# An S4 layer with a gated feed-forward on one core: the same 2006 tasks in another order

## The chip, the core and the metric

The kernel runs on one core of a Trainium2 chip. The metric is the device time of one execution in microseconds. It is read beside a profile of one further execution, which gives what each engine did: TensorE (PE, matrix products), VectorE (DVE), ScalarE (ACT), GpSimd (POOL) and SyncE (SP), which here does nothing but issue DMA transfers.

## The reference, cut to what matters

```python
x = A_u                                            # 2048 tokens x 448 channels
sa, ca, ga, sb, cb, gb = (silu(c) @ w_mod) in six parts
h = layernorm(x) * (1 + ca) + sa
# S4 convolution of h, channel by channel
dt = exp(log_dt)
K = real(einsum("dn,dnl,dn->dl", C, exp(dt * A * l), dt * B))   # 256 states, 2048 taps
y = irfft(rfft(pad(h)) * rfft(pad(K)))[:2048] + h * Dskip
x = x + ga * y
h = layernorm(x) * (1 + cb) + sb
# GeGLU: 448 -> 1792 -> 448
x = x + gb * ((gelu(h @ w_gate) * (h @ w_up)) @ w_down)
```

## The kernel before, in words

**Stages.** The kernel has four parts that overlap in time.

1. *Normalisation and transform of the input.* The input is normalised (tasks `bn`, `norm`), and its Fourier transform over the 2048 taps is made in two matrix stages (`ua`, `ub`) with evictions from PSUM (`ua.ev`, `ub.ev`) and a trip through DRAM between them.
2. *Generation of the convolution kernel.* The 448 channels are cut into 56 pieces of 8, each with 256 states. A piece needs two exponential factors (PE tasks `x.mm` L638 and `y.mm` L657 with ACT exponentials L644 and L662), angles (`ang`, `anc`, PE L675), their magnitude (`mag`: ACT L680 or DVE L683), sine and cosine on ACT (L688, L692, L699), two products on DVE (`tx` L721, 1.22 us; `tyc` L725, 2.29 us) and then the generation matmuls on PE (`kgen`, L748). Two pieces make one tile that is evicted (`kev`, ACT or DVE), corrected with the skip term (`kd`, L766), transformed by PE (`ka`, L771) and evicted again (`kout`, ACT or DVE). The coefficients that this needs come from a chain of small DVE and ACT operations on `in_abc` (tasks `p.*`), turned through DRAM.
3. *The convolution.* For two of three channel groups PE transforms the kernel (`f.fwd`, L1094), DVE multiplies with the input's transform (`f.pr`, L1098), PE transforms back (`f.inv`, L1105), and the result goes to DRAM. The third group is done at the end by other shapes (`t.fwd` L1189, DVE combinations `t.p0`, `t.p1` at L1197 and L1200, `t.inv` L1207, `t.i0` L1216, stores L1224 and turned reads `yi.l0`, `yi.l1` at L1297). The last inverse stage, token block by token block, is `co.mm*` (PE, L1404 and L1409) with the residual and second normalisation behind it.
4. *The feed-forward*, for four blocks of 512 tokens and 14 tiles of 128 hidden channels. A task `gu` (PE L1530, with a 64-row part at L1524) makes gate and up of one tile; ACT applies the GELU (L1537), DVE multiplies (L1544), and the hidden values are split in a high and a low half (L1556, L1559). The down products (`dn`, PE L1599 and L1630) follow after each block. The gate/up weights are split once (`w.hi`, `w.lo`), kept in DRAM as `w_d`, and for blocks 1 to 3 read back by `wr.ld` (L1367, 896 KB each, on SP) into a ring of three slots; one load serves two `gu` tasks. The down weights arrive by `d.ld` and `e.ld` (L1737) and share a ring of two buffers (`fq`) with the products of gate and up.

**What sets the order.** Every piece of work is a task. A task is added with a name, the engines that can do it, a function that issues its instructions, and the tasks it depends on. A table `PLACE` gives each task a rank, one number for the whole kernel; where a task can run on several engines a letter behind the rank picks one (a ACT, d DVE, p POOL, s SP). `Plan.order` (with an assertion that every task stands behind those it depends on) sorts by rank, and `Plan.run` lets the tasks issue their instructions in that order:

```python
    def order(self):
        out = sorted(self.tasks, key=lambda t: t.at)
```

Each engine takes its instructions strictly in the order in which they were issued to it. So the rank sets, at the same time, the order on every engine, which buffer of a ring a task gets, and in which order transfers enter SP's queue. The ranks are no times: an engine waits in front of a task until its inputs and its buffer are there, and everything behind it on that engine waits too. Instructions of PE come in several tile shapes (rows by columns of the array that a matmul uses): 64x128 for `x.mm`, `y.mm` and `ang`, 128x32 for `kgen`, 128x64 for `ka` and `co.mm*`, 128x128 for the transforms and most of `gu`.

Of the kernel before, what the change touches and what calls it, by code (L numbers as in the profile page):

```python
# [40 lines left out]
    "anc": "120 138 145 163 157 200 209 244 266 311 327 339 347 355 438 456 470 487 499 524",  # L41
    "ang": "108 112 126 149 151 169 204 212 241 298 319 324 341 350 421 443 454 476 496 506 511 591 602 610 654 670 690 698 "
        "741 761 764 775 792 795 805 885 894 905 908 927 932 950 1007 1018 1021 1034 1039 1051 1115 1124 1135 1151 1157 1169 "
        "1187 1197",
    "as": "67d 80a 99d 109d 114d 128d 156a 185a 250d 258d 265a 289d 309d 333d 334d 365d",
    "bn": "48 49 60 58 41 50 51 53 227 243 235 239 187 224 197 210",
    "c.ai": "1257",
    "c.ak": "5",
    "c.au": "4",
    "c.c": "2",  # L50
    "c.ea": "20",
    "c.ih": "1283",
    "c.ld": "7",
    "c.rd": "22",
    "c.t1": "219",
    "co.adde": "1329 1347 1366 1355",
    "co.addl": "1384 1387 1421 1410",
    "co.addx": "1495 1510 1499 1522 1676 1716 1739 1688 1799 1811 1817 1809",
    "co.ca": "1404a 1408a 1456a 1441a",
    "co.cb": "1415d 1416a 1459a 1448a",  # L60
    "co.h0": "1398a 1403a 1447d 1430a",
    "co.h2": "1534a 1579a 1571a 1561a 1752a 1748d 1759a 1765d 1856d 1889a 1841a 1873a",
    "co.l0": "1402 1405 1449 1434",
    "co.l2": "1541 1584 1573 1576 1753 1754 1763 1766 1857 1893 1851 1884",
    "co.mme": "1321 1341 1336 1346",
    "co.mml": "1381 1382 1409 1407",
    "co.mmx": "1492 1506 1494 1509 1640 1703 1735 1649 1792 1805 1812 1796",
    "co.n": "1392 1399 1438 1425",
    "co.nx": "1527 1574 1548 1532 1749 1746 1751 1764 1829 1875 1837 1870",
    "co.rc": "1390 1397 1431 1423",  # L70
    "co.rcx": "1525 1743 1828",
    "co.rt": "1388 1393 1424 1418",
    "co.rtx": "1524 1741 1818",
    "co.xt": "1541 1584 1573 1576 1753 1754 1763 1766 1857 1893 1857 1884",
    "co.ta": "1401 1406 1453 1436",
    "co.tb": "1411 1413 1454 1439",
    "cos": "523 609 623 635 689 694 715 708 760 774 794 791 804 819 817 893 906 912 930 946 949 963 1016 1028 1040 1050 1057 "
        "1066 1129 1134 1155 1175 1180 1196 1207 1220",
    "cos2": "124 146 147 167 165 207 213 254 273 321 332 342 349 359 445 462 485 492 502 531",
    "d.hi": "1566 1547 1583 1496 1533 1600 1504",  # L80
    "d.ld": "1555 1538 1569 1484 1516 1585 1491",
    "d.lo": "1567 1552 1587 1501 1535 1602 1514",
    "d0": "13",
    "dn": "1603 1605 1607 1613",
    "dn.k0": "1742 1891 1994",
    "dn.k2": "1755 1896 2000",
    "dn.k3": "1757 1899 2002",
    "dn.r": "1606 1608 1614 1634",
    "dn.r1": "1745 1963 2008",
    "dn.r4": "1768 1903 2004",  # L90
    "dn.r5": "1770 1909 2010",
    "dn.r6": "1778 1908",
    "dn.rh": "2005 2012 2016",
    "dn.s0": "2015",
    "dn.s1": "2017",
    "dn.st": "1657 1658 1620 1639 1747 1780 1775 1779 2007 1952 1950 1948 2014 2006 2013",
    "dn0": "1726 1737 1880 1885 1986 1992",
    "dn1": "1738 1887 1993",
    "dn2": "1767 1902 2003",
    "dn3": "1772 1905",  # L100
    "dn3h": "2009 2011",
    "dn4": "1750 1897 1999",
    "dn5": "1744 1894 1998",
    "dn6": "1761 1898 2001",
    "dsk": "178",
    "dt": "26",
    "e.f": "1666 1718 1704 1615 1650 1628 1685",
    "e.hi": "1668 1720 1708 1617 1653 1631 1689",
    "e.ld": "1656 1705 1696 1610 1638 1619 1675",
    "e.lo": "1671 1723 1710 1618 1655 1636 1691",  # L110
    "ev.end": "1253",
    "ev.fp": "707",
    "ev.geg": "1445",
    "ev.pq": "1328",
    "ev.ps": "1437",
    "ev.ub": "389",
    "ev.w0": "1339",
    "f.fc": "714 716 754 773 801 823 851 880 895 917 942 1015 1030 1052 1071 1094 1114 1137 1158 1189",
    "f.fwd": "738 753 783 806 832 855 879 902 924 947 969 998 1014 1036 1055 1077 1098 1120 1141 1162 1209 1216",
    "f.inv": "750 768 796 815 847 865 889 911 936 960 983 1010 1026 1046 1067 1089 1108 1130 1154 1176 1226 1232",  # L120
    "f.pr": "743 759 790 812 839 859 884 907 931 953 975 1002 1020 1041 1060 1083 1101 1125 1149 1167 1212 1225",
    "f.st": "763 782 809 830 897 878 904 929 977 1000 1009 1023 1042 1079 1090 1106 1131 1148 1168 1193 1243 1240",
    "f.ut": "710 721 755 776 803 826 854 870 901 918 944 966 988 1017 1032 1054 1073 1097 1123 1138 1160 1182",
    "f.z": "758a 778d 802a 829a 868a 871d 896d 926a 952d 979a 1005d 1019a 1038d 1061a 1085a 1102a 1128d 1143a 1163a 1188a "
        "1235a 1239a",
    "gs": "70 110",
    "gu": "1480 1497 1511 1519 1528 1539 1549 1560 1570 1578 1596 1616 1622 1632 1644 1651 1660 1669 1678 1686 1694 1706 "
        "1712 1721 1777 1781 1784 1798 1800 1808 1816 1822 1830 1838 1843 1852 1859 1869 1907 1910 1913 1919 1924 1931 1935 "
        "1941 1945 1958 1964 1970 1974 1981",
    "gu.g": "1429 1450 1458 1465 1468 1471 1474 1481 1502 1508 1521 1529 1540 1550 1562 1572 1581 1595 1604 1623 1633 1641 "  # L130
        "1654 1661 1670 1679 1687 1695 1709 1713 1722 1727 1782 1785 1793 1801 1806 1813 1824 1831 1839 1844 1853 1860 1874 "
        "1878 1911 1914 1920 1925 1932 1936 1942 1946 1959 1965 1972 1975 1982 1987",
    "gu.h0": "1475 1485 1515 1536 1557 1580 1599",
    "gu.ha": "1626 1647 1663 1682 1698 1717 1730 1787 1804 1819 1835 1849 1864 1882 1917 1933 1943 1953 1967 1977 1989",
    "gu.hs": "1629 1646 1667 1690 1701 1732 1734 1794 1820 1826 1846 1862 1871 1888 1923 1930 1955 1957 1983 1979 1996",
    "gu.l0": "1478 1488 1517 1544 1558 1582 1601",
    "gu.la": "1635 1648 1672 1684 1700 1725 1733 1789 1825 1834 1855 1854 1866 1883 1918 1939 1956 1961 1968 1984 1990",
    "gu.ls": "1630 1652 1673 1693 1702 1740 1736 1797 1821 1840 1850 1865 1872 1890 1929 1940 1971 1960 1995 1980 1997",
    "gu.m": "1432 1452 1460 1466 1469 1472 1476 1483 1505 1513 1526 1531 1545 1554 1564 1575 1591 1597 1609 1625 1637 1643 "
        "1659 1662 1674 1681 1692 1697 1711 1715 1724 1729 1783 1786 1795 1803 1807 1815 1827 1833 1842 1847 1858 1863 1876 "  # L140
        "1881 1912 1916 1921 1927 1934 1938 1944 1949 1962 1966 1973 1976 1985 1988",
    "gu.s": "1627 1645 1664 1683 1699 1719 1731 1788 1810 1823 1836 1848 1867 1886 1922 1928 1951 1954 1969 1978 1991",
    "gu2": "1420 1427 1442 1457 1464 1467 1470 1473",
    "ka": "216 272 306 363 374 409 465 519 570 606 711 719 745 800 836 887 920 954 957 989 1063 1070 1127 1174 1190 1224 "
        "1245 1250",
    "kd": "205 249 304 352 371 403 459 515 559 582 675 697 742 789 820 883 913 939 951 984 1047 1068 1119 1172 1185 1211 "
        "1241 1248",
    "kev": "191d 238d 285d 351d 368d 401d 431d 497a 551d 579d 661a 680d 737d 786a 816a 856a 890d 922a 948d 980d 1045d 1065a "
        "1104d 1146a 1183d 1198a 1219a 1246a",
    "kgen": "142 175 189 223 257 280 294 322 329 357 387 396 418 424 480 491 513 546 534 574 620 641 659 673 724 731 757 779 "  # L150
        "788 810 828 841 857 874 898 916 933 941 965 974 1003 1029 1043 1059 1081 1100 1117 1139 1145 1164 1181 1195 1204 "
        "1213 1238 1242",
    "kout": "247a 288a 318a 377d 448a 414a 505a 530a 583d 634d 720d 733d 771a 811a 843a 892d 928a 962a 992a 993d 1076a 1110d "
        "1142a 1177a 1200a 1228a 1251d 1252a",
    "lt0": "55 136 317 358 568 766 860 955",
    "lt1": "87 173 335 393 696 833 971 995",
    "m.cp": "532d 589a 818d",
    "m.cp0": "40d",
    "m.ev": "63 68 47 545 598 838",
    "m.ld": "6 19 12 423 539 727",  # L160
    "m.mm": "45 57",
    "m.mq": "527 581 772",
# [1671 lines left out]
```

## Time and profile before

| what | value |
|---|---|
| median of 3 runs | 787.75 us (787.74 to 788.98) |
| profiled execution, its own time | 787.92 us |
| span of the profiled execution | 786.1 us |
| mean granted TensorE clock | 0.991 |
| busy: PE, DVE, ACT | 728.7, 591.4, 460.1 us |
| moved by DMA | 139.88 MB |

How to read it: the span is the time from the first to the last recorded instruction. Busy time is what an engine spent on instructions; its share of the span is an average over stages with different limits, so the prediction reads it by stretches of 40 us. The chain of waits starts at the last instruction and goes back at each step to what released it. The ends of matmuls are modelled, and instructions in a row overlap in the list by 0.07 to 0.16 us, so that sums of durations come out a little above the time they take.

### The profile page before, as it was taken

How to read it: one execution, taken by the hardware profiler on the slowest of the kernel's cores; microseconds unless marked ns; L12 is line 12 of the kernel's file. 1: busy time of each engine (PE TensorE's matmuls, PEld its weight loads, DVE VectorE, ACT ScalarE, POOL GpSimd, SP SyncE). 2: the span in 40 equal slices, each digit the busy share in tenths (PEclk: the TensorE clock that was granted, in tenths of full speed). 3: DMA queues.
4: the chain of work that ended last, by engine and by line, in shares of the span. 5: the costliest groups of instructions: out<-in, count | busy, mean ns of one | idle time of the engine just before them, and what ended most of it. 6: DMA issues, size and time to landing. Idle time of an engine off the chain costs nothing.

```text
span 786.1 us, 19037 instructions
## 1 busy us (share of the span) xinstructions
PE 728.7 (93%) x8166; PEld 445.2 (57%) x8166; DVE 591.4 (75%) x891; ACT 460.1 (59%) x613; POOL 9.0 (1%) x24
## 2 busy tenths in 40 slices
PE   1876889998899999989999999999999999999998
PEld 0333454543667767778784445444595446944478
DVE  4889999999999999988768851469773587134743
ACT  5699999899999999961554730233421244012320
POOL 0000000000000000000300000000000000000000
PEclk9899999999999999999999999999999999999999
DMA  9555558997887767999797884345437324012201
GB/s 265 157 156 145 155 140 249 277 277 227 240 259 216 224 190 216 285 300 251 192 312 221 274 219 146 129 134 186 161 67 213 104 94 134 14 48 94 82 2 60
DMA packets 103791, 139.88 MB, mean 178 GB/s; under 512 B 34388, under 2 KB 85268, under 8 KB 103706
## 3 DMA queue, kind: packets, MB, share of 16 engines
q1 hardware_dynamic: 97828, 130.47, 56.7%
q10 hardware_dynamic: 5318, 7.22, 2.9%
q8 instruction: 64, 1.05, 0.5%
q0 software_dynamic: 560, 0.98, 0.4%
q14 instruction: 21, 0.17, 0.1%
HBM read 100.39 MB, written 36.01 MB: 174 GB/s over the span
## 4 chain that ended last, share of the span: by engine, by line
PE 67%; ACT 13%; DVE 9%; DMA 7%; issue 3%; SPq 1%; ACTq 0%; DVEq 0%
PE pq L1530 29%; PE pq L1630 9%; PE pd L1599 4%; PE kg L748 3%; PE pf L1105 3%; PE pg L675 3%; ACT my L662 2%; DVE ty L725 2%; PE pf L1094 2%; ACT fg L688 2%; PE pq L1524 2%; PE kg L771 2%; DMA yi<-y 2%; PE pd L1630 2%; PE pf L984 1%
## 5 line engine op out<-in xcount | busy, mean ns | idle before, releaser
L1530 PE MATMUL pq<-ht,wr 128*128 128x512 f16 (+1 forms) x1200 | 248.3, 365 | 0.1
L1530 PEld LDWEIGHTS <-wr 128*128 128x128 f16 x1200 | 114.7, 98 | 128.4 <-issue 11.3
L725 DVE TENSOR_TENSOR ty<-my,fg 128x2048 f32<-128x2048 f32 x56 | 127.6, 2285 | 0.9 <-ACT fg L699 0.3
L1537 ACT ACTIVATE ge<-pq 128x512 f32<-128x512 f32 (+1 forms) x60 | 33.9, 566 | 106.4 <-PE pq L1524 71.2
L1544 DVE TENSOR_TENSOR fq<-ge,pq 128x512 f32<-128x512 f32 (+1 forms) x60 | 39.0, 649 | 73.0 <-PE pq L1530 46.1
L1556 ACT ACTIVATE hh<-fq 128x1024 f16<-128x1024 f32 (+1 forms) x49 | 46.7, 961 | 63.9 <-DVE fq L1544 45.3
L721 DVE TENSOR_TENSOR tx<-mx,fg 128x1024 f32<-128x1024 f32 x56 | 67.7, 1219 | 1.8 <-ACT fg L692 1.0
L1630 PE MATMUL pq<-d,hh 128*128 128x224 f16 x476 | 68.9, 259 | 0.0
L748 PE MATMUL kg<-ty,tx 128*32 128x64 f32 x3584 | 62.5, 221 | 4.0 <-issue 2.3
L748 PEld LDWEIGHTS kg<-ty,tx 128*32 128x32 f32 x3584 | 53.0, 110 | 22.7 <-issue 14.7
L1559 DVE TENSOR_TENSOR hlo<-fq,hh 128x1024 f16<-128x1024 f32 (+1 forms) x49 | 53.7, 1106 | 12.9 <-ACT hh L1556 12.7
L1630 PE MATMUL pq<-d,hlo 128*128 128x224 f16 x238 | 61.6, 259 | 0.0
L688 ACT ACTIVATE fg<-pg 128x1024 f32<-128x1024 f32 x56 | 58.1, 1038 | 0.8 <-PE pg L675 0.4
L662 ACT ACTIVATE my<-pg 128x1024 f32<-128x1024 f32 x56 | 55.9, 1032 | 2.6 <-PE pg L657 2.2
L1630 PEld LDWEIGHTS <-hh 128*128 128x128 f16 x560 | 54.2, 98 | 0.9 <-issue 0.2
L1105 PE MATMUL pf<-q,fc 128*128 128x160 f32 x264 | 41.5, 307 | 1.2 <-DVE q L1098 1.2
L692 ACT ACTIVATE fg<-fg,small 128x1024 f32<-128x1024 f32 x36 | 41.5, 1170 | 0.1
L1105 PEld LDWEIGHTS pf<-q,fc 128*128 128x128 f32 x264 | 36.4, 190 | 6.6 <-issue 1.5
L675 PEld LDWEIGHTS <-lt 64*128 64x128 bf16 x304 | 17.9, 95 | 39.0 <-issue 27.0
L675 PE MATMUL pg<-ea,lt 64*128 64x512 bf16 x152 | 30.7, 391 | 8.4 <-ACT fg L699 3.2
L1747 ACT ACTIVATE d<-fq 128x896 f16<-128x896 f32 x14 | 13.2, 946 | 41.7 <-PE pd L1599 27.3
L984 PE MATMUL pf<-ui,fu 128*128 128x448 f32 x66 | 31.0, 575 | 1.9 <-ACT uo L480 1.4
(209 smaller groups left out, 1122.6 us busy)
## 6 DMA issues: line engine op xcount, KB each, us to landing
wr<-w_d SPq DMA_DIRECT2D x21, 896.0 KB
fc<-in_k_fc SPq DMA_DIRECT2D x20, 576.0 KB
u_d<-so SPq DMA_DIRECT2D x32, 224.0 KB
ui<-u_d SPq DMA_DIRECT2D x10, 672.0 KB
fq<-in_wd SPq DMA_DIRECT2D x14, 448.0 KB
w<-in_wgu SPq DMA_DIRECT2D x11, 512.0 KB
us<-uo SPq DMA_DIRECT2D x22, 240.0 KB
q<-us SPq DMA_DIRECT2D x22, 240.0 KB
```

The source lines that it names most:

```text
L662: A.activation(yb.tile.rearrange("p h (n k) -> p n h k", n=2), pb.tile.rearrange("p (n h k) -> p n h k", n=2, h=2), AF.Exp)
L675: T.matmul(pa[:, nh * 512:nh * 512 + 512], w, x, start=(k == 0), stop=(k == 2))
L688: A.activation(fb.tile[:, 0].rearrange("p x (n k) -> p n x k", n=2), pb.tile.rearrange("p (n x k) -> p n x k", n=2, x=2), AF.Sin, scale=TW ...
L692: A.activation(fb.tile[:, 1], fb.tile[:, 1], AF.Sin, scale=-TWO_PI, bias=halfpi)
L721: V.tensor_mul(tx.tile, xb.tile[:, xm, None, :].to_broadcast([128, 2, 512]), fb.tile[:, :, 0])
L725: V.tensor_mul(ty.tile, yb.tile[:, :, None, :].to_broadcast([128, 2, 2, 512]), fb.tile[:, None, :, 1].to_broadcast([128, 2, 2, 512]))
L748: T.matmul(kg[32 * g:32 * g + 32, 2 * (s % 2) + q, :64], tx[:, r, nh, 4 * q + g], ty[:, 0:4:3, nh, 4 * q + g] if r else ty[:, 1:3, nh, 4 * ...
L1105: T.matmul(pz.tile[:, e % 32 - sl0], fc.tile[:, i, 1 + t], pp.tile[:, t, i], start=(t == 0 and e != 32), stop=(t == 1 and e != 0))
L1530: T.matmul(pb.tile[k][:, ts], wr.tile[:, 4 * lo + t, k, c0:c0 + 128], ht[:, m, ts], start=f % 2 == 0 and i == 0, stop=f % 2 == 1 and i == 9)
L1556: A.activation(hg.tile[0][:, cb, c], fq.tile[:, c], AF.Copy)
L1559: V.tensor_sub(hg.tile[1][:, cb, c], fq.tile[:, c], hg.tile[0][:, cb, c])
L1630: T.matmul(bank(k)[:, m], x[:, p, q[0], ts], w[:, p, q[1]], start=new and m == 0 and p == 0 and z == 0, skip_group_check=True, stop=i in ( ...
```

## The change

Only the table `PLACE` changes; of its entries nearly all do. Nothing else differs: the same 2006 tasks, the same 5630 matmuls, 389 transfers on SP's queue in both, 43 loads of ACT's function tables in both. 221 lines of the table differ. The new order was searched with a model in which a change of tile shape on TensorE costs time and each operation counts with its own measured duration. The core of the diff, with the rows that the prediction speaks of:

```diff
 PLACE = {
...
-    "co.mmx": "1492 1506 1494 1509 1640 1703 1735 1649 1792 1805 1812 1796",
...
-    "e.ld": "1656 1705 1696 1610 1638 1619 1675",
...
-    "p.D1": "24 141 420 597",
...
-    "w.le": "1285 1344 1323",
-    "wr.ld": "1563 1611 1621 1624 1642 1677 1680 1707 1714 1728 1791 1802 1814 1832 1845 1861 1879 1915 1926 1937 1947",
...
-    "x.ld": "18 8 201 139",
...
-    "yi.ld": "1463 1598 1776",
...
+    "co.mmx": "1497 1518 1529 1496 1656 1686 1674 1679 1776 1812 1816 1774",
...
+    "e.ld": "1676 1726 1690 1611 1615 1643 1683",
...
+    "p.D1": "37 153 419 568",
...
+    "w.le": "1279 1290 1280",
+    "wr.ld": "1604 1584 1626 1624 1660 1655 1706 1703 1775 1729 1805 1789 1830 1841 1829 1907 1868 1924 1910 1947 1959",
...
+    "x.ld": "38 1 198 145",
...
+    "yi.ld": "1468 1609 1768",
```

By the letters, 13 more of the 28 `kev` run on ACT, 4 more of the 36 `mag` on DVE, 4 more of the 28 `kout` on ACT (3 of them ahead of the last product); some `ua.ev`, `ub.ev`, `f.z` (evictions) and `co.h2` change sides too. In PE's order two tasks in a row have different tile shapes 340 times before and 296 times now.

Two places of the order follow. First PE, in the generation, before: a `ka` task (L771), two `y.mm` tasks (L657, the number in `pg` tells the task, and each has two load and matmul pairs), an `f.fwd` (L1094), a lone `y.mm`, and a `kgen` (L748).

```order
L771 MATMUL kg_3673<-ak_111,ke_3773 64x128 x8
L657 LDWEIGHTS lt_3219
L657 MATMUL pg_3810<-ea_109,lt_3219 128x512
...
L657 MATMUL pg_3815<-ea_109,lt_3219 128x512
...
L1094 MATMUL pf_3824<-ako_2560,fc_3603 128x160 x3
L657 LDWEIGHTS lt_3219
L657 MATMUL pg_3831<-ea_109,lt_3219 128x512
...
L748 MATMUL kg_3836<-ty_3788,tx_3722 32x64 x32
```

The lone `y.mm` between two other shapes makes two changes of shape.

The same engine a little further on, in the new order: two `kgen` tasks, of which the second is shown, `f.inv` (L1105) and `f.fwd` (L1094), both 128x128, then two `y.mm` and a `ka`.

```order
L748 MATMUL kg_4043<-ty_4027,tx_4000 32x64 x32
L1105 MATMUL pf_4110<-q_3995,fc_4025 128x160 x6
L1094 MATMUL pf_4128<-ako_2539,fc_4123 128x160 x3
L657 LDWEIGHTS lt_4029
L657 MATMUL pg_4135<-ea_109,lt_4029 128x512
...
L657 MATMUL pg_4138<-ea_109,lt_4029 128x512
...
L771 MATMUL kg_3883<-ak_111,ke_3992 64x128 x8
```

Tasks of one shape now stand together more often: six tasks here with three changes of shape between them.

Second SP's queue in blocks 0 and 1 of the feed-forward, where the ring of gate/up weights (L1367) shares it with the down weights (L1737), the reads of the convolution's result (L1278) and the stores of finished rows (L1610). Before:

```order
L1278 DMA yi<-y_69 64x2x512 x2
L1737 DMA fq<-in_wd 128x4x224
L1367 DMA wr<-w_d 128x3584
L1359 DMA w_d<-wr 128x3584
L1737 DMA fq<-in_wd 128x4x224
L1610 DMA out<-x_5033 128x448
L1367 DMA wr<-w_d 128x3584 x2
```

Now:

```order
L1278 DMA yi<-y_69 64x2x512 x2
L1737 DMA fq<-in_wd 128x4x224 x2
L1367 DMA wr<-w_d 128x3584 x2
L1610 DMA out<-x_5089 128x448
L1737 DMA fq<-in_wd 128x4x224
L1610 DMA out<-x_5089 128x448 x3
L1367 DMA wr<-w_d 128x3584 x2
```

Two down-weight loads now stand ahead of two ring loads, the second of which (`wr.ld` 2) is for the fifth `gu` task of block 1 (`gu` 14) and gets the slot that `gu` 11 frees; before, the slot of each ring load was freed four or more `gu` tasks ahead of its use.

428 rows, old and new, of the table PLACE are left out of this document.

## The prediction

> **What bounds the kernel now.** I read the profile in four steps: the busy table, the busy time by stretches of 40 us, the chain of waits that ended last, and then single places in the timeline. The busy table says only that TensorE (PE) is the busiest engine, with the vector engine (DVE) next:
>
> ```profile
> PE 728.7 (93%) x8166; PEld 445.2 (57%) x8166; DVE 591.4 (75%) x891; ACT 460.1 (59%) x613; POOL 9.0 (1%) x24
> ```
>
> An average over 786.1 us hides the stages, so the stretches come next (columns: busy us of PE, of its weight loads, of DVE, ACT and POOL, each with the number of instructions; granted clock; DMA share; GB/s):
>
> ```profile
> 0.00:40.00 40.00, 18.88 (x58) 8.38 (x60) 27.02 (x61) 23.73 (x37) 1.52 (x11) 0.94 0.73 213
> 40.00:80.00 40.00, 27.50 (x416) 13.49 (x414) 37.33 (x59) 39.13 (x50) 0.00 (x0) 0.97 0.52 150
> 80.00:120.00 40.00, 35.62 (x712) 20.12 (x709) 39.30 (x55) 39.71 (x51) 0.00 (x0) 0.97 0.54 149
> 120.00:160.00 40.00, 38.36 (x635) 18.81 (x633) 39.41 (x50) 35.49 (x53) 0.00 (x0) 1.00 0.92 263
> 160.00:200.00 40.00, 34.38 (x482) 16.27 (x480) 37.77 (x50) 39.78 (x51) 0.00 (x0) 0.99 0.89 254
> 200.00:240.00 40.00, 38.55 (x760) 27.96 (x756) 39.68 (x38) 38.23 (x46) 0.00 (x0) 0.97 0.82 241
> 240.00:280.00 40.00, 39.60 (x778) 29.94 (x777) 37.78 (x43) 38.75 (x45) 0.00 (x0) 1.00 0.79 222
> 280.00:320.00 40.00, 39.31 (x702) 29.77 (x704) 37.86 (x40) 38.60 (x44) 0.00 (x0) 1.00 0.71 215
> 320.00:360.00 40.00, 35.89 (x815) 28.84 (x815) 35.84 (x39) 27.53 (x36) 0.00 (x0) 1.00 0.94 304
> 360.00:400.00 40.00, 38.38 (x422) 31.72 (x416) 34.96 (x74) 20.11 (x41) 7.52 (x13) 1.00 0.82 229
> 480.00:760.00 280.00, 280.00 (x1720) 157.12 (x1719) 163.06 (x294) 81.27 (x113) 0.00 (x0) 1.00 0.34 104
> ```
>
> There are three regimes. Up to 200 us PE idles (it is busy 34 to 38 us of 40 at best) while DVE and ACT are nearly full: those two make the operands of the kernel generation. From 200 to 320 us all three stand between 37.8 and 39.7: none has room. From 480 us PE is busy without a gap, so there only PE's own work counts. The chain of waits ties them together (start, length, engine, tile, line):
>
> ```profile
> 349.81 1.23 DVE tx L721
> 351.09 1.10 PE kg L748 x64
> ...
> 375.90 6.17 DMA w<-in_wgu
> 382.08 2.45 DMA yi<-yb_d
> 392.44 2.34 PE pq L1530 x20
> ...
> 431.15 8.74 PE pq L1530 x40
> ...
> 440.43 8.74 PE pq L1530 x40
> ```
>
> The last product of the generation (DVE, L721) feeds the last generation matmuls (L748) at 351.09, which end at 352.19; the third channel group's transform and the first block's output convolution follow; the gate/up matmuls (L1530) start at 392.44, run at 9.28 us for two tasks (431.15 to 440.43) and PE never rests long again. So three things can move the end: the time of the last L748 (351), the length of the tail from there to 392, and PE's work plus stalls after 392.
>
> **The change part by part.** No operation, transfer or buffer comes or goes; tasks change places, and some change engine. I cost what the new places do.
>
> *TensorE's changes of tile shape.* What one costs is read from neighbours of the same kind:
>
> ```profile
> 277.70 0.39 PE L657 MATMUL pg<-ea,lt 64*128 64x512 bf16 x2
> 278.02 0.44 PE L771 MATMUL kg<-ak,ke 128*64 128x128 f32 x4
> ...
> 308.31 0.61 PE L657 MATMUL pg<-ea,lt 64*128 64x512 bf16 x4
> 308.85 0.40 PE L1094 MATMUL pf<-ako,fc 128*128 128x160 f32 x1
> ```
>
> A lone exponent task (two matmuls) ahead of another shape holds PE from 277.70 to 278.02, 0.32 us; two in a row hold it from 308.31 to 308.85, 0.54 us instead of 0.64. One change spared is worth 0.10 us. The two orders hold 340 changes and 296. What matters is where. Between the 25th of the 56 generation tasks, near the start of the window 200:240, and the last they hold 133 and 115: 18 fewer, 1.8 us of PE in the stage where it is as full as the others. Eleven of the rest go before that, where PE waits for DVE and ACT anyway, and seven in the tail, where it waits for DVE: nothing. The last eight are counted with the gate/up part. The Trainium skill warns (Perfetto Trace Analysis, "Tensor Engine Instruction (MATMUL, LD_WEIGHTS)") that the end of a matmul in a trace is estimated, not observed. By that rule a price from ends could be an artefact, and the sum would lose this term and come out at 786.7; mine compares starts, so I keep it.
>
> *DVE and ACT in the same stage.* The 1.8 us can only be had if DVE delivers 1.8 us sooner, as it has no more idle time than PE has. The two orders place evictions and magnitudes differently. DVE's groups (mean ns):
>
> ```profile
> L482 DVE COPY ke<-kg 128x252 f32<-128x252 f32 x17 | 7.0, 412 | 0.2
> L683 DVE TENSOR_SCALAR fg<-pg 128x1024 int32<-128x1024 int32 x6 | 7.3, 1220 | 0.9 <-PE pg L675 0.9
> L482 DVE COPY ako<-kg 128x512 f32<-128x512 f32 x9 | 6.2, 685 | 1.3 <-PE kg L771 1.3
> ```
>
> Ahead of the last product DVE loses 13 of the first (5.3 us) and 3 of the third (2.1 us), gains 4 of the second (4.9 us); summed in this way over all kinds, with each task's own duration, DVE has 2.5 us less to do up to its last product, and ACT 1.4 us more up to its last cosine, where ACT ends long before (27.5 of 40 busy in 320:360). Where the new order differs most on the way, at generation tasks 15 and 18, DVE's work is 7 us less and then 7.6 us more, PE's likewise; from task 24 on it is 1 to 3 us less throughout. I take the smaller of the two, PE's 1.8 us. The bounds: PE idles 6.7 us between 200 and 360 and 1.6 us in 360:400, so at best 8.3 us more; in the other direction one more wait like those in the chain.
>
> *Start.* The new order loads a second 896 KB input tile before the constants and defers one reciprocal that stood ahead of the first coefficient transpose:
>
> ```profile
> L574 DVE RECIPROCAL q<-q 112x256 f32<-112x256 f32 x4 | 7.0, 1753 | 0.1
> 709.00:710.00 1.00, 1.00 (x6) 0.45 (x5) 0.97 (x4) 0.00 (x0) 0.00 (x0) 1.00 0.95 186
> 710.00:711.00 1.00, 1.00 (x6) 0.49 (x5) 1.00 (x2) 0.54 (x1) 0.00 (x0) 1.00 0.97 401
> 711.00:712.00 1.00, 1.00 (x7) 0.39 (x4) 0.56 (x1) 0.51 (x1) 0.00 (x0) 1.00 0.77 323
> ```
>
> The reciprocal is 1.75 us earlier for the transpose; the tile, 918 kB, takes 2.3 us of the DMA engines at the 401 GB/s of the fullest microsecond of such a load. They cancel: 0, between -1.8 and +2.3.
>
> *Tail, 352 to 392.* Here DVE's 27 combinations at about 0.7 us each decide, and their number and first input are the same. What changes is SP's queue: the last weight loads (L1332) now stand ahead of the reads of the turned third group (L1297), which in the chain above waited for just such a load (375.90, 6.17 us, then 2.45 us). Walking the queues I find the same end within a microsecond: 0, between -1 and +6.2.
>
> *Gate/up and down.* Of the eight output-convolution pieces (L1404, L1409) for token blocks 2 and 3, six stood alone between gate/up or down tasks; now the eight form four pairs, three more than before.
>
> ```profile
> 513.88 0.76 PE L1404 MATMUL pd<-yi,ai 128*64 128x320 f32 x4
> 514.47 0.39 PE L1409 MATMUL pd<-yi,ai 128*64 128x128 f32 x4
> 514.79 4.49 PE L1530 MATMUL pq<-ht,wr 128*128 128x512 f16 x20
> ...
> 606.41 0.76 PE L1404 MATMUL pd<-yi,ai 128*64 128x320 f32 x4
> 607.00 0.39 PE L1409 MATMUL pd<-yi,ai 128*64 128x128 f32 x4
> ...
> 608.08 0.39 PE L1524 MATMUL pq<-ht,wr 64*128 64x512 f16 x2
> ```
>
> Alone a piece takes 0.91 us (513.88 to 514.79), two take 1.67 (606.41 to 608.08): 0.15 saved, and 0.10 for the change back that falls away. Three more pairs: 0.75 us, all on the path. Of the pieces for block 1, one waited for its input:
>
> ```profile
> 417.47 0.76 PE L1404 MATMUL pd<-yi,ai 128*64 128x320 f32 x4
> 418.58 0.44 PE L1409 MATMUL pd<-yi,ai 128*64 128x128 f32 x4 [0.36 <-DMA yi<-y]
> ```
>
> Undisturbed, its second part comes 0.59 us after the first (606.41 to 607.00), here 1.11: 0.5 us of stall. The new order issues that load ahead of other loads, some 2.5 us sooner: 0.5 gained, bounds 0 and 0.6.
>
> The price on the other side is in the weight ring. It has three slots; a load of 896 KB is issued when a gate/up task pair has freed a slot. Before, at least four such tasks (18 us) lay between release and use; now in four places only two, 9.3 us. A lone load takes 4 us: issued at 708.07 as below, its bytes have moved by 712, as the rows of 709 to 712 above show. So 5 us remain.
>
> ```profile
> 708.07 0.32 SPq L1367 DMA_DIRECT2D wr<-w_d  x1
> ...
> L1747 ACT ACTIVATE d<-fq 128x896 f16<-128x896 f32 x14 | 13.2, 946 | 41.7 <-PE pd L1599 27.3 <-DVE fq L1744 7.8 <-DMA fq<-in_wd 6.7
> ```
>
> The narrowest place is block 1: two ring loads stand in SP's queue behind a load of down weights that waits for DVE to free its buffer. From PE's start of that block I count: task done at 4.6, then, with an estimate of 3 us, its evictions and DVE's four differences to 7.6, ACT's cast of 0.95 us to 8.5, DVE's remainder, about as long, to 9.6, then three loads of 2.24 MB together, 5.6 us at 401 GB/s after about 1 us: landed at about 16.5, needed after four tasks at 18.6. No stall, with 2 us to spare. On this count the Trainium skill (DMA: Bandwidth & Descriptors, "Queues, rings and completion order") says that descriptors are consumed in ring order, which would make the load needed first the last of the three; no row here shows that for three at once.
>
> **Sum.** The profiled execution took 787.92 us (span 786.1), within 0.2 us of the median of 787.75. 787.9 - 1.8 - 0.75 - 0.5 = 784.9 us.
>
> **Rivals.** (A) The order also closes gaps. For it: the 8.3 us of PE idle time in 200 to 400, and the idle 2.2 us of DVE in each of the windows from 240. Against: three engines are above 94% there at once, and the tail is a chain of dependences. Half of the gaps gone gives 784.9 - 4.2 = 780.7; all, 776.6. (B) The spared changes are not on the path: DVE and ACT, which lead to 351.09, keep their idle times, and in the later part the gain is only the pairs: 787.9 - 0.75 = 787.2. For it: DVE's 39.7 of 40 in 200:240. Against: DVE has less work too. (C) Slower: in the tail the reads of the turned third group fall behind the weight loads once more. SP issues in order, and a transfer that waits for its predecessor's completion holds all behind it. The chain shows the price of one such wait, 6.17 us; it decides when the wait ends after DVE's combinations do, at about 385. Then 784.9 + 6.2 = 791.1; with half of it covered, 788.0, which would be no change; the ring loads of block 1, if 5 us late instead of 2 us early, would give a similar time.
>
> **How the numbers follow.** Forecast as above, between -1.6 and -6 us, 0.43: 784.9. A 0.15, B 0.21, C 0.21. A run of this kernel tells 0.2%, 1.6 us, from no change: faster is below 786.2. The forecast and A are faster, 0.58; B is within, 0.21; C slower, 0.21. The range reaches down to A with nearly all gaps closed and up to C with nearly the whole wait, 777.5 to 790.5, and leaves about a tenth out on each side.
>
> **What would show it.** Right: the last L748 ends at about 350.4 instead of 352.19, PE idles as much as before between 200 and 360, the first L1530 at about 390.6 instead of 392.44, no row of L1409 with a wait on yi, PE busy 280.00 of 280 from 480. Wrong on the first term: the last L748 at the old time, with PE idle grown by what the changes spared. C shows as a wait of PE or DVE on yi<-yb_d around 385, or as PE idle at an L1530 behind wr<-w_d after 490. The forecast fails altogether if DVE's or ACT's idle time in 40 to 320 us, 10.9 and 10.3 us now, changes by several us either way: that I could not work out, since it hangs on hundreds of meetings of two queues.

## The result and the profile after

| kernel | time, us | ratio to before, 95% interval |
|---|---|---|
| before, on the same chip | 788.18 (787.74 to 788.98) | 1 |
| the change | 824.18 (822.35 to 826.4) | 1.0457 [1.0427, 1.0486] |

The change makes the kernel 36.0 us slower, where 784.9 was forecast and 790.5 was the upper end. The profiled execution took 826.4 us (span 824.6). Its busy table, of which the prediction showed the one before:

```profile
PE 739.1 (90%) x8166; PEld 453.1 (55%) x8166; DVE 590.7 (72%) x888; ACT 459.7 (56%) x616; POOL 9.1 (1%) x24
```

DVE and ACT have as much to do as before, within 0.7 us; PE has 10.4 us more for the same 8166 instructions. The stretches of 40 us from 40 to 360 us, and one from 480 to 760 (columns as in the prediction), show where the time lies:

```profile
40.00:80.00 40.00, 28.22 (x383) 13.92 (x381) 33.21 (x54) 32.60 (x41) 0.00 (x0) 0.83 0.54 148
80.00:120.00 40.00, 34.65 (x570) 19.04 (x572) 34.88 (x51) 35.95 (x48) 0.00 (x0) 0.87 0.37 103
120.00:160.00 40.00, 34.59 (x636) 18.00 (x635) 37.07 (x38) 37.31 (x55) 0.00 (x0) 1.00 0.83 239
160.00:200.00 40.00, 33.20 (x468) 15.12 (x460) 34.03 (x46) 33.28 (x45) 0.00 (x0) 0.96 0.89 249
200.00:240.00 40.00, 35.81 (x628) 22.52 (x624) 35.46 (x40) 36.51 (x45) 0.00 (x0) 0.91 0.80 230
240.00:280.00 40.00, 35.24 (x740) 27.06 (x730) 35.49 (x35) 35.91 (x44) 0.00 (x0) 1.00 0.65 191
280.00:320.00 40.00, 36.52 (x668) 27.97 (x668) 36.16 (x38) 35.68 (x42) 0.00 (x0) 1.00 0.71 192
320.00:360.00 40.00, 36.92 (x709) 29.00 (x698) 32.21 (x32) 33.32 (x41) 0.00 (x0) 0.91 0.77 231
480.00:760.00 280.00, 279.88 (x1695) 154.77 (x1693) 169.63 (x312) 80.21 (x111) 0.00 (x0) 1.00 0.45 137
```

Behind 480 us nothing has changed: PE is busy 279.88 of 280. Ahead of 360 us no engine is full any more. From 80 to 320 us, where DVE and ACT stood at 35.5 to 39.8 of 40, all three now stand between 33 and 37.3. In one stretch over the whole stage, first before and then after, the prediction's 10.9 and 10.3 us of idle time read as follows.

```profile
40.00:320.00 280.00, 253.33 (x4474) 156.37 (x4472) 269.12 (x328) 269.71 (x332) 0.00 (x0) 0.98 0.74 213
```

```profile
40.00:320.00 280.00, 238.24 (x4041) 143.64 (x4043) 246.31 (x295) 247.25 (x315) 0.00 (x0) 0.94 0.68 193
```

DVE idles 280 - 246.31 = 33.7 us there and ACT 32.8, three times as much as before, and the granted clock falls from 0.98 to 0.94. Up to the end of DVE's last product (L721), before and then after, the same reads:

```profile
0.00:351.10 351.10, 300.21 (x5200) 186.32 (x5201) 327.24 (x416) 319.99 (x402) 1.52 (x11) 0.98 0.75 220
```

```profile
0.00:386.20 386.20, 310.33 (x5138) 194.55 (x5140) 323.54 (x407) 320.20 (x410) 1.59 (x11) 0.93 0.69 198
```

DVE has 3.7 us less to do up to there, and idles 62.7 us instead of 23.9.

Milestones from both traces split the loss (end of a task, us):

| task | before | after | difference |
|---|---|---|---|
| first `kgen` | 52.0 | 56.7 | +4.8 |
| 14th | 126.5 | 136.7 | +10.2 |
| 28th | 219.5 | 235.8 | +16.3 |
| 42nd | 291.0 | 315.1 | +24.1 |
| 56th, the last L748 | 352.2 | 389.5 | +37.3 |
| first 64-row gate/up task (L1524) | 395.0 | 434.5 | +39.5 |
| from there to the last down product | 387.6 | 386.6 | -1.0 |

So the loss grows all through the generation of the convolution kernel, by 10.2, 6.1, 7.8 and 13.2 us in its four quarters. The tail behind it costs 2.2 us more and the feed-forward 1.0 us less.

What the engines wait for in that stage tells more. The waits of DVE from 40 to 390 us (tile, line, what it waited for: us in total, times, longest), before and after:

```profile
DVE ke L766 <- ACT ke L480: 1.6, 1, 1.6
```

```profile
DVE ke L766 <- ACT ke L480: 21.0, 8, 6.0
DVE q L1098 <- PE pf L1094: 8.6, 4, 6.1
```

Those of ACT, after:

```profile
ACT my L662 <- PE pg L657: 8.6, 5, 5.4
ACT fg L688 <- DVE fg L683: 8.0, 8, 2.0
```

Those of PE, after:

```profile
PE kg L748 <- DVE ty L725: 7.1, 5, 4.5
PE kg L748 <- issue: 4.4, 2, 3.1
```

Each engine waits for each of the others. The largest group is an operation of 0.17 us, `kd` (L766), which adds the skip term to a tile that ACT has evicted. One such meeting in the timeline after (start, length, engine, line, operation, with the idle time before it in brackets):

```profile
370.18 1.28 ACT L688 ACT_TABLE_LOAD   x1
371.48 1.02 ACT L688 ACTIVATE fg<-pg 128x1024 f32<-128x1024 f32 x1
372.39 1.14 ACT L692 ACTIVATE fg<-fg,small 128x1024 f32<-128x1024 f32 x1
373.43 0.37 ACT L480 ACTIVATE ke<-kg 128x252 f32<-128x252 f32 x1
...
373.84 0.17 DVE L766 TENSOR_TENSOR ke<-kg,d 128x4 f32<-128x4 f32 x1 [6.01 <-ACT ke L480]
373.91 2.28 DVE L725 TENSOR_TENSOR ty<-my,fg 128x2048 f32<-128x2048 f32 x1
...
376.11 1.22 DVE L721 TENSOR_TENSOR tx<-mx,fg 128x1024 f32<-128x1024 f32 x1
...
376.34 0.97 PE L748 MATMUL kg<-ty,tx 128*32 128x64 f32 x27 [4.47 <-DVE ty L725]
```

The eviction (L480) stands behind a table load, a sine and a cosine on ACT. `kd` stands ahead of two products on DVE and holds them for 6.01 us; the sine and cosine that the first of them needs had ended at 362.9. The generation matmuls that need the products then come 4.47 us late on PE. No task there is longer than it was; the heads of the queues wait for one another.

### The profile page after: what moved, and what is told of

It is laid out like the page before. It is cut to its first block, busy times and chain, and to the rows that moved or that the text cites. A ratio compares the mean times of both kernels' runs of the same rounds, so it can differ in the third digit from the quotient of the medians.

```text
span 824.6 us, 19048 instructions
## 1 busy us (share of the span) xinstructions
PE 739.1 (90%) x8166; PEld 453.1 (55%) x8166; DVE 590.7 (72%) x888; ACT 459.7 (56%) x616; POOL 9.1 (1%) x24
## 4 chain that ended last, share of the span: by engine, by line
PE 43%; DVE 2%; DMA 2%; issue 1%; ACT 1%; SPq 1%; ACTq 0%; DVEq 0%
PE pq L1530 26%; PE pq L1630 8%; PE pd L1599 4%; PE pq L1524 2%; PE pd L1630 1%; DMA fq<-in_wd 1%; DMA w<-in_wgu 1%; PE pf L1207 1%; PE pd L1404 1%; DMA yb_d<-z 1%; SPq L1297 0%; ACT wr L1345 0%; DVE wr L1349 0%; DVE fq L1544 0%; DVE my L1200 0%
## 5 line engine op out<-in xcount | busy, mean ns | idle before, releaser
L748 PE MATMUL kg<-ty,tx 128*32 128x64 f32 x3584 | 66.7, 234 | 17.3 <-DVE ty L725 7.1
L748 PEld LDWEIGHTS kg<-ty,tx 128*32 128x32 f32 x3584 | 58.6, 119 | 35.4 <-issue 21.9
L721 DVE TENSOR_TENSOR tx<-mx,fg 128x1024 f32<-128x1024 f32 x56 | 68.0, 1218 | 5.9 <-ACT my L662 2.5
L1105 PE MATMUL pf<-q,fc 128*128 128x160 f32 x264 | 42.6, 317 | 0.0
L1105 PEld LDWEIGHTS pf<-q,fc 128*128 128x128 f32 x264 | 38.5, 199 | 4.1 <-issue 2.6
L771 PE MATMUL kg<-ak,ke 128*64 128x128 f32 x448 | 32.3, 290 | 5.8 <-DVE ke L766 4.6
L675 PEld LDWEIGHTS <-lt 64*128 64x128 bf16 x304 | 17.5, 97 | 32.6 <-issue 20.0
```

The source lines that it names most:

```text
L675: T.matmul(pa[:, nh * 512:nh * 512 + 512], w, x, start=(k == 0), stop=(k == 2))
L721: V.tensor_mul(tx.tile, xb.tile[:, xm, None, :].to_broadcast([128, 2, 512]), fb.tile[:, :, 0])
L748: T.matmul(kg[32 * g:32 * g + 32, 2 * (s % 2) + q, :64], tx[:, r, nh, 4 * q + g], ty[:, 0:4:3, nh, 4 * q + g] if r else ty[:, 1:3, nh, 4 * ...
L1105: T.matmul(pz.tile[:, e % 32 - sl0], fc.tile[:, i, 1 + t], pp.tile[:, t, i], start=(t == 0 and e != 32), stop=(t == 1 and e != 0))
```

## Experiments: which part of the table does it

The change is one table, so the first question is which half of it costs, ranks or engine letters. Two kernels take one half from each table. `OLD` and `NEW` are the two tables; the first kernel takes the new ranks and the old letters:

```diff
-        at = PLACE[n][i]
-        self.at, e = int(at.rstrip("adps")), at[-1]
+        self.at, e = int(NEW[n][i].rstrip("adps")), OLD[n][i][-1]
```

> All tasks at their new places, but on the engines that they had before (evictions kev mostly back on DVE, and so on). The kernel before is at 788, the change at 824. Theory E (the changed engines make the loss: 13 evictions kev moved to ACT, so that DVE stands at kd, 21 us instead of 1.6, until ACT comes to them): the waits at L766 fall to a few us and the time to about 800. Theory P (the places make it: on each engine a task now stands ahead of work that could run, whatever the engine): 818 to 826, with the waits moved to other lines.

Measured: 850.98 us beside 791.08 for the kernel before in the same series (one execution each; 791.08 is some 3 us above that kernel's median, so only large differences count here). The last L748 ended at 411.5, 59.4 us late. That is outside both expectations. The second kernel has the two exchanged:

```diff
+        self.at, e = int(OLD[n][i].rstrip("adps")), NEW[n][i][-1]
```

> The reverse: all tasks at their places of before, on the new engines. Theory E: 800 to 812, with DVE waiting at L766 for 15 us or more. Theory P: 787 to 795.

Measured: 810.2 us, the last L748 at 372.0, 19.8 us late, with DVE waiting 11.2 us at the line that is L766 of the change. Neither half is the culprit by itself: the new ranks lose more with the old letters (850.98 - 791.08 = 59.9 us) than with their own (36.0), and the old ranks lose 19.1 us (810.2 - 791.08) with the new letters. The two halves do not add up; a rank and a letter have to be chosen together.

## Experiments: which stretch of the program does it

Hybrids run one order up to a task and the other behind it. For the first the core of the edit is this, and the others only exchange the tables or the task:

```diff
-        out = sorted(self.tasks, key=lambda t: t.at)
+        first = sorted(self.tasks, key=lambda t: rank(t, t.old))
+        k = next(i for i, t in enumerate(first) if (t.n, t.no) == ("kgen", 55)) + 1
+        out = first[:k] + sorted(set(first[k:]), key=lambda t: (rank(t, t.new), self.tasks.index(t)))
```

Old until the last `kgen`, new behind it:

> Order and engines of before up to the last generation matmul, the new ones for all that is left then (tail and feed-forward). Both theories put the loss in the generation: the last L748 near 352, time 786 to 790. If the new order of tail and feed-forward is worth what the prediction said (0.75 for the pairs and 0.5 for the wait), 786.5 to 787.5 unless the tail gives it back; the changed kernel's tail from the last L748 to the first L1530 was 2 us longer than before.

Measured: 790.89 us beside 791.08. The last L748 ended at 351.3, the first 64-row gate/up task at 398.6: in this profile the new tail takes 47.3 us instead of 42.8, and the new feed-forward 387.0 instead of 387.6. The reverse, new until the last `kgen`:

> The reverse: new order and engines up to the last generation matmul, those of before for what is left. Both theories: last L748 near 389 as in the change, time 822 to 826. A time under 815 would say that the tail and the feed-forward have a good part of the loss.

Measured: 827.64 us, the last L748 at 387.6. As far as single executions tell, all of the loss is in the generation. The old tail, behind the new generation, took 47.0 us here, so the 47.3 above can't be put down to the tail's new order. Then the generation itself was cut in the middle. New through the 28th `kgen`, old behind it:

```diff
+        first = sorted(self.tasks, key=lambda t: rank(t, t.new))
+        k = next(i for i, t in enumerate(first) if (t.n, t.no) == ("kgen", 27)) + 1
```

> New order and engines up to the 28th of the 56 generation matmul tasks, those of before for what is left then. In the changed kernel this task was 16 us late, the last one 37 us. If the loss is spread evenly and each stretch adds its own: 800 to 808. If it comes from the start alone (constants, first coefficient transposes): 820 and more.

Measured: 809.31 us beside 788.54. The drift (how much later a `kgen` ends than the one of the same number before the change) was 16.3 us at the 28th, 19.7 at the 42nd and 20.6 at the last. Once the old order runs again, it loses no more than 4 us behind the seam of the two orders. And old through the 28th:

> The reverse of the run before: order of before up to the 28th generation task, the new one from there. Spread evenly: 805 to 812, the 28th task near 220 as before, the last one near 372. From the start alone: 787 to 792.

Measured: 810.24 us. The drift was 0.2 us at the 28th `kgen` and 19.6 at the last. The halves cost 20.8 and 21.7 us (809.31 and 810.24 less 788.54). So the loss is not one bad place: each half of the generation makes its own, and together they come to a few us more than the change loses.

## Experiments: the longest wait, and the clock

The wait at L766 was the longest group, 21.0 us. In the next kernel each of the 28 `kd` moves back behind up to three other tasks on DVE, as far as nothing that needs it is passed:

```diff
+        for t in [t for t in out if t.n == "kd"]:
+            i = out.index(t)
+            k = next(j for j in range(i + 1, len(out)) if t in out[j].deps)
+            behind = [j for j in range(i + 1, k) if out[j].on == "DVE"][:3]
+            if behind:
+                out.insert(behind[-1], out.pop(i))
```

> The changed kernel (824), with each of the 28 tasks kd (0.16 us on DVE) moved behind up to three DVE tasks that stand behind it in the new order, as far as its reader allows. Theory W (DVE stands at a small task whose input ACT delivers late, and that starves everything behind it): the waits at L766, 21 us, fall under 8 and the time to 800 to 814. Theory D (the order as a whole doesn't fit, and a wait removed at one place comes up at another): L766 falls too, but the time stays above 818.

Measured: 819.96 us (815.27 to 821.39), ratio 1.0388 [1.035, 1.0425]. DVE's waits in this kernel, whose lines stand 6 lower (L772 is L766 of the change):

```profile
DVE q L1104 <- PE pf L1100: 8.5, 5, 5.0
DVE ke L772 <- ACT ke L486: 6.3, 6, 2.0
DVE uo L998 <- PE pf L990: 5.4, 3, 4.7
```

The wait fell by 14.7 us, the time by 4.2. Another group came up, at an eviction (L998), and the wait at L1104 stayed. Most of all, PE now waits for the `kd` that were moved back (L777 is L771 of the change, where it waited 3.8 us, 4 times):

```profile
PE kg L777 <- DVE ke L772: 15.9, 10, 3.9
```

So for 14.7 us of waiting that went on DVE, 12.1 came up on PE. Taking away the longest wait by rule gives back little, because the rule makes those wait who need the task that it moves.

The second suspect is the clock. Mean granted clock and span of the profiled executions give what it lost: (1 - 0.967) x 824.6 = 27.2 us after, (1 - 0.991) x 786.1 = 7.1 us before. Matmuls whose results are overwritten at once were put ahead of four tasks in front of which PE waits and behind which the clock is halved; they add work and leave nothing out:

```diff
+    def keep(n, dst, w):
+        for _ in range(n):
+            T.matmul(dst, ea[:, :128], ea[:, 512:512 + w], start=True, stop=True)
...
+            keep({51: 35, 52: 50}.get(s, 0), kg[:, 2 * (s % 2):2 * (s % 2) + 2, :64], 128)
...
+                keep({8: 12}.get(4 * jb + j, 0), pbs[0].tile, D)
...
+                keep({25: 6}.get(e0 + i, 0), pb.tile, D)
```

> The changed kernel with matmuls on constants, overwritten at once, in front of four tasks for which PE waited 2.1 to 4.5 us: ua 8 (12 of them), ub 25 (6), kgen 51 (35) and kgen 52 (50). They fill PE while it waits and change nothing else. In the changed kernel PE ran at half clock for 54 us of the first 400, in pieces of 3.4 us behind such waits. Theory C (the halved clock is a good part of the loss): 4 to 8 of the 16 pieces are gone and the time is 816 to 820. Theory W or D alone (PE is not what the others wait for): 822 to 828, PE's added work costing as much as it gains.

Measured: 820.53 us (820.24 to 821.25), ratio 1.0407 [1.0381, 1.0433]. Two of the stretches, which had 0.87 and 0.91:

```profile
80.00:120.00 40.00, 31.51 (x582) 17.65 (x581) 37.40 (x53) 38.29 (x52) 0.00 (x0) 1.00 0.42 114
320.00:360.00 40.00, 38.31 (x837) 29.90 (x837) 35.85 (x35) 37.90 (x46) 0.00 (x0) 1.00 0.86 256
```

The clock is full there now; in all it loses (1 - 0.979) x 818.6 = 17.2 us, 10.0 less. The time fell by 3.7, a tenth of the loss. What was gained at 80 us was lost again by the 28th `kgen` (drift 16.8 us, in the change 16.3); what was gained late stayed: from the 42nd to the last `kgen` the drift grows by 6.2 us instead of 13.2.

## Experiments: the meetings of the queues

If the order on one engine makes the heads of the queues wait, then changing that order alone, with everything else left as the change has it, must give a large part back. With the durations of the trace I followed DVE's queue and found the tasks that wait while the one behind them is ready. DVE passes over such a task 48 times, at 35 places: 18 of them up to the end of the generation, at eight of which a `kd` goes back, and 17 later. PE's order with its 296 changes of shape, ACT's and SP's order and all letters stay. As an example, the tasks around the meeting shown above, in the order of DVE's queue:

```diff
-kd.25  tyc.52  tx.53  f.pr.21  f.pr.20  tyc.54
+tyc.52  tx.53  f.pr.21  f.pr.20  tyc.54  kd.25
```

> The changed kernel with 48 pairs of tasks that are neighbours in DVE's queue swapped: in each the first stands waiting for another engine while the second is ready. TensorE's order, with its 296 changes of shape, every task's engine and all of the computation stay as in the changed kernel. Theory that in-order queues set the loss (a waiting task holds what is ready behind it): DVE's idle time between 40 and 320 us falls from 33.7 us by at least 10, the last L748 ends below 375 instead of 389.5, and the time is 795 to 810. Theory that waits only come up elsewhere, as they did when 28 corrections of the skip term moved: 816 to 822. Theory that the granted clock alone makes the loss: the time follows the low clock, 824 less about 0.4 us for each us of clock regained, 818 or more. Theory that TensorE's new order itself is at fault, whatever DVE does: 820 to 826.

Measured: 807.46 us (804.21 to 812.21) beside 789.96, ratio 1.0229 [1.0185, 1.0274]. DVE's wait from 40 to 390 us (its line is 30 higher up here), and three stretches:

```profile
DVE ke L736 <- ACT ke L450: 7.2, 8, 2.3
```

```profile
40.00:320.00 280.00, 242.06 (x4156) 147.60 (x4155) 251.83 (x300) 252.10 (x321) 0.00 (x0) 0.95 0.71 198
320.00:390.00 70.00, 63.45 (x1280) 51.38 (x1280) 61.85 (x70) 49.85 (x69) 0.54 (x1) 1.00 0.87 267
80.00:120.00 40.00, 35.25 (x580) 19.73 (x581) 37.30 (x53) 37.13 (x50) 0.00 (x0) 0.87 0.39 108
```

Half of the loss is gone, 2.28 of 4.57 per cent, by the order of one engine. The last L748 of the change is at 370.5 instead of 389.5. One expectation failed: from 40 to 320 us DVE's idle time fell by 5.5 us only (280 - 251.83 = 28.2), not by 10. The larger part of the gain lies from 320 to 390, where DVE is busy 61.85 of 70; in the change that stretch read:

```profile
320.00:390.00 70.00, 57.34 (x1193) 46.01 (x1182) 51.64 (x49) 50.41 (x63) 0.00 (x0) 0.88 0.72 210
```

The 17 later places add nothing: from the first 64-row gate/up task to the last down product this kernel takes 386.7 us, the change 386.6. The clock improved along with the waits (loss 18.6 us instead of 27.2), so some of the gain came through the clock; at the rate of the kernel with the filled waits (3.7 us for 10.0) that would be, as an estimate, 3 us of the 16.7. It can be more: from the 42nd to the last `kgen` the drift grows by 13.2 us in the change, by 6.2 with the filled waits and by 0.5 with the swaps, and in both of these the clock is full from 320 to 390 us. So, by these single profiles, up to 7 us of the late gain could be had through the clock alone, and the other 5.7 only by the swaps.

The same kernel with matmuls that fill PE's waits at two places of the first 90 us:

```diff
+                keep({2: 5, 8: 12}.get(4 * jb + j, 0), pbs[0].tile, D)
```

> The kernel with 48 neighbouring pairs swapped in DVE's queue (807.46 us) plus idle-filling matmuls on TensorE: 5 ahead of the third matmul task of the input's first transform stage (L891 there) and 12 ahead of the ninth, each 128x448, written to a tile that the real matmul then overwrites; they add work and leave nothing out. TensorE waits there 1.34 and 3.66 us, and the clock is halved behind it at 36 to 43 and 80 to 91 us (8.5 of the 18.8 us of clock that this kernel loses up to 440 us). If the clock early on sets the remaining 18 us: the stretches at 36 and 80 vanish, the drift at the 14th generation task, +8.5 us against before, falls to +3 or less, and the time is 800 to 803. If the clock there is lost beside waits that last as long anyway: the stretches vanish, the 14th generation task moves by less than 2 us, and the time is 805 to 809.

Measured: 802.87 us (801.66 to 804.91) beside 788.47, ratio 1.0173 [1.0142, 1.0204]. Its stretch from 80 to 120 us, where the kernel with the swaps alone had 37.30 of DVE and a clock of 0.87:

```profile
80.00:120.00 40.00, 33.80 (x671) 19.38 (x671) 39.29 (x54) 39.49 (x54) 0.00 (x0) 0.98 0.49 136
```

The 14th `kgen` ended 3.3 us later than before the change instead of 8.5, and the 5 us held through the 41st. The slow stretch at 80 us is gone, the one at 36 only became shorter. This fits the first expectation nearly: early on, where PE's first transform stage feeds the rest, the clock does set the time, and 17 matmuls that compute nothing bring 4.6 us (the clock's loss in all falls by 3.3 us, to 15.3). What is left, 14.4 us, is open: its drift grows between the 28th `kgen` (+5.9 us) and the 49th (+17.5), with DVE waiting 8.5 us for L1094's results in the list of its waits, and no run separates that further.

## Experiment: the feed-forward alone

The part of the prediction that came out can be had alone: the order of before through the first 64-row gate/up task, the new one behind it.

```diff
+        k = next(i for i, t in enumerate(first) if (t.n, t.no) == ("gu2", 0)) + 1
```

> The order and engines of before up to and with the first 64-row gate/up task (L1524 for the hidden channels above 1664 of block 0), those of the change behind it; all of the computation stays. The terms of the prediction for this part say -0.75 (three more pairs of output-convolution pieces) and -0.5 (the load of the first pieces issued sooner): 786.9 beside 788.2 of the kernel before, and between 786.5 and 787.7 as the changed kernel took 386.6 us from its first such task to the end, the one before 387.6. If the ring loads stall TensorE after all: over 789. If the gain was noise of two profiles: within 0.3 us of before.

Measured: 789.02 us (785.6 to 790.48, 12 executions) beside 789.96 (17), ratio 0.9987 [0.997, 1.0004]. The likeliest value is the expected gain of 1 us, but the interval includes no change, and in its profile the part from that task to the last down product took 387.5 us, as before the change (387.6), because 0.9 us was lost behind the seam, in the first 70 us. All profiles together speak for a smaller gain: this part took 386.3 to 387.5 us in the six with the new order there and 387.4 to 387.7 in the three with the old one, some 0.6 us on average. Still, no kernel here can be said to beat the one before.

## Why the prediction was wrong

**What held.** The three regimes were read rightly: what happens behind 395 us comes out as PE's own work. The eight output-convolution pieces form four pairs, and each takes 1.66 or 1.67 us, as was worked out. So does the first pair of block 1, where the stall had been:

```profile
461.69 0.76 PE L1404 MATMUL pd<-yi,ai 128*64 128x320 f32 x4
462.28 0.39 PE L1409 MATMUL pd<-yi,ai 128*64 128x128 f32 x4
462.50 0.71 PE L1404 MATMUL pd<-yi,ai 128*64 128x320 f32 x4
463.04 0.39 PE L1409 MATMUL pd<-yi,ai 128*64 128x128 f32 x4
463.36 4.49 PE L1530 MATMUL pq<-ht,wr 128*128 128x512 f16 x20
```

It holds PE from 461.69 to 463.36, 1.67 us, and the first piece's second part comes 0.59 us after its first, so the stall on `yi` is gone. Pairs and stall were put at -0.75 and -0.5 together; the feed-forward took 1.0 us less in the profile. The ring loads of block 1 stall nothing (279.88 of 280 above), as the count said.

The tail, put at 0 between -1 and +6.2, measured +2.2. PE's wait at the end of it, before and after:

```profile
PE pd L1409 <- DMA yi<-yb_d: 1.0, 1, 1.0
```

```profile
PE pd L1409 <- DMA my<-in_k_ft: 2.0, 1, 2.0
```

It is 1 us longer, a small piece of the 6.17 us that rival C put there. The transfer named differs; the hybrids with the new tail alone and with the old tail behind the new generation wait there 3.0 and 2.6 us, so the tail's order alone doesn't decide it.

**What failed first.** The start was put at 0, between -1.8 and +2.3. The first and last start of the generation's weight loads, before and after (smallest, median and largest length in ns ahead of them):

```profile
L748 PEld LDWEIGHTS kg<-ty,tx x3584: 106/110/110, 50.9 to 351.9; 128*32 128x32 f32 x200
```

```profile
L748 PEld LDWEIGHTS kg<-ty,tx x3584: 105/110/178, 54.8 to 389.2; 128*32 128x32 f32 x200
```

They start 3.9 us later, outside the bounds: only a load and a reciprocal were costed there, not the order of the rest. It is not where the time went, though: the fourth `kgen` is on time again, 0.1 us ahead of before.

**The step that failed.** It is "*DVE and ACT in the same stage*": "I take the smaller of the two, PE's 1.8 us", with "one more wait like those in the chain" as the bound in the other direction. The sums behind it were right: up to its last product DVE had 3.7 us less to do (2.5 had been worked out), and ACT's work there stayed within 0.3 us. But the step turned less work into less time, and that holds only while idle time stays as it was. DVE's idle time up to its last product grew by 38.8 us, so the product ended 35.1 us later; in 40 to 320 us DVE's and ACT's grew by 22.8 and 22.5 us. The bound was mis-sized, too. It priced one more wait, 6.2 us; DVE alone now has eight at L766, 21.0 us. Nor had the sum a term for the clock, which lost 27.2 us instead of 7.1. Where the engines are so nearly full (all three above 94% from 200 to 320 us before), a wait of one becomes a wait of the next, as at the meeting shown above; there is little slack to take it. The two halves of the generation, which cost 20.8 and 21.7 us when only one has the new order, show that the price is paid in both. That the order of DVE's queue is behind it is shown for half of the loss; of the rest, 14.4 us stay open.

The text had named the condition itself: the forecast "fails altogether" if that idle time "changes by several us either way", and it said that it could not work this out. It then gave that case no mechanism and no share of its own. Of the rivals, C was on the right side at the wrong place, with a sixth of the size. A rival "the queues no longer fit", with its place in the generation, should have stood there, and the range should have taken it in. The row of three nearly full engines was read as having no room for a gain beyond PE's changes; it also says how much there is to lose.

**The changes of shape.** Whether the 18 spared changes brought their 1.8 us cannot be seen under a loss of 37 us. It was not tried alone.

## What to carry to other kernels

Where several in-order engines are nearly full together, the idle time is a result of the order, not a constant: a sum of work saved says nothing until each queue's head has been followed against the others. A new order is best judged by the list of waits, engine by engine, and a small operation that waits at the head of a full queue (0.17 us that waited 6.01) costs what stands behind it. Moving it by rule can make those wait who need its result. When the table of an order changes everywhere, hybrids of both orders find the stretch that costs, and an exchange on one engine alone shows whether it is the meeting of the queues.

## What the runs showed of the hardware

Short waits cost more than their length, because TensorE's clock falls behind them. After the change two `kgen` tasks stand in a row, the second waits 3.08 us, and the `f.inv` (L1105) behind it runs at half speed:

```profile
319.36 1.76 PE L748 MATMUL kg<-ty,tx 128*32 128x64 f32 x111
324.21 0.74 PE L748 MATMUL kg<-ty,tx 128*32 128x64 f32 x17 [3.08 <-issue]
324.88 3.57 PE L1105 MATMUL pf<-q,fc 128*128 128x160 f32 x12
328.24 1.81 PE L1094 MATMUL pf<-ako,fc 128*128 128x160 f32 x6
```

The same kind of task before the change:

```profile
283.25 1.90 PE L1105 MATMUL pf<-q,fc 128*128 128x160 f32 x12
```

The stretches around it after the change, with the granted clock as the third number from the end:

```profile
322.00:324.00 2.00, 0.00 (x0) 0.00 (x0) 2.00 (x1) 1.98 (x4) 0.00 (x0) 0.81 0.56 165
324.00:326.00 2.00, 1.79 (x21) 1.63 (x22) 0.03 (x1) 1.28 (x1) 0.00 (x0) 0.50 0.83 203
326.00:328.00 2.00, 2.00 (x10) 2.00 (x9) 0.00 (x0) 0.00 (x0) 0.00 (x0) 0.50 0.59 178
328.00:330.00 2.00, 2.00 (x10) 1.67 (x11) 0.00 (x0) 0.00 (x0) 0.00 (x0) 0.50 0.66 113
330.00:332.00 2.00, 2.00 (x24) 1.40 (x24) 1.92 (x3) 1.35 (x2) 0.00 (x0) 0.98 0.64 251
```

The clock is 0.50 from about 323.2 to 330.1, twice 3.4 us, and PE works without a gap from 324.2 on; so the `f.inv` takes 3.57 us instead of 1.90. A piece of 3.4 us at 0.50 loses 1.7 us; the 7.1 and 27.2 us lost in the two executions make four pieces before the change and sixteen after it. The Trainium skill (TensorE: Matmul & The Clock Gate, "Part 1: The HAM clock gate (the "warmup" mystery)") has the clock at half behind an idle window of about 3.4 us and a window that runs free of the program. The trace agrees on 0.50 and on the length. A part of it goes beyond that section: after the swaps, the clock fell at 36.0 us although PE's longest wait in the 3.4 us before was 1.34 us, and PE was busy 1.55 of these 3.40 us (0.44 in the 1.70 us from 33.1).

What the 3.08 us wait is, the list of waits does not say: it names only PE's own issue, twice for 4.4 us in this stage (before the change three times for 2.3), and DVE's products for this task had ended at 317.01 and 319.21. The DMA records say more. The queue q8, of the kind `instruction`, moves 64 pieces of 16 KiB in every trace but one, and 65 in the one with 103 matmuls added; that is one piece for about 256 of PE's 16332 matmuls and weight loads, so it is taken here for PE's own program. One piece ran from 321.68 to 322.78, and PE went on at 324.21, 1.43 us behind it. It is the same at all 18 waits of more than 0.6 us inside a `kgen` task in the thirteen traces: each ends 1.27 to 1.65 us behind the end of such a piece. So PE very probably waited for its next instructions: two `kgen` tasks in a row hold 256 of them and take 2.2 us, and one piece takes about 1 us to arrive. No run changed this alone.
